# A graph kernel on one core: every second scatter burst as four 128x32 matmuls a step, and half of a table entry made one tile later

## The chip, the cores and the metric

The kernel runs on one core of a Trainium2 chip. The metric is the device time of one launch in microseconds. The granted TensorE clock is read from the profile of the same execution.

## What is computed

The reference propagates node features seven times along the edges of a random graph (10,000 nodes, 160,000 edges, 128 features), then runs a small attention over the eight versions of each node. The change touches the propagation alone:

```python
h = x                                   # (10000, 128)
toks = [x]
for _ in range(7):
    msg = h[src] * deg_inv_sqrt[src, None] * deg_inv_sqrt[dst, None]
    h = segment_sum(msg, dst, 10000)    # sum of the messages by destination node
    toks.append(h)
tok = stack(toks, axis=1)               # (N, 8, D), then attention, residual, readout
```

## The kernel before

The nodes are cut into 79 tiles of 128. A first stage sorts the edges by cells and builds, for each destination tile, a set of 0/1 matrices in fp8 that is kept in DRAM (`GSd`) and loaded into a tile `w`. Each hop is then matrix work. The features of all nodes lie in SBUF as a table `tab` of f16 values; an entry is 256 wide, a high half and a low half, which together hold a 32-bit value closely enough. There are two such tables, one that a hop reads and one that it writes; a copy in DRAM (`tabd`, and `tabh` for the last seven tiles) serves the few edges that are fetched by index.

Hops 2 to 7 run in the second part of `run`. For each destination tile `block` does the following.

- `gather` (nine calls a tile, L608): four 128x32 matrices of `w`, side by side in the four column groups of TensorE, pick up to 32 rows each out of four source tiles into a quarter of a PSUM tile `p`. A call makes two such groups, so a tile has 18 groups, 72 matmuls. The pool of `p` has six buffers. ScalarE (L613) evacuates five of the nine `p` tiles and VectorE (L615) four, into f16 tiles `eb`.
- `begin` opens the accumulator `acc` with the rows that were fetched by index (`fetched`, L568: two full 128x128 matrices).
- `scat` (L583) multiplies the gathered rows by full 128x128 matrices of `w` and adds them up in `acc`, two matmuls for each `eb`.
- `close` adds the two halves of `acc` on VectorE (L599, the tile `s`) and calls `fin`.

The order on TensorE follows from the list `pend`: a scatter is put there when its gather is issued, and when a tile's nine gathers are out, the list is emptied down to two. So TensorE sees bursts: 72 gather matmuls of one tile, then 20 scatter matmuls (two of `begin`, the last four products of the tile before, and the first fourteen of this one), then the gathers of the next tile. The places in a hop's order are numbered n = 0 to 78 (tiles 72 to 78 first, then 0 to 71).

`fin` makes the new table entry of a finished tile in `entries`: ScalarE writes the high half (L644), VectorE the low half (L645), which is the value less the high half, and the maximum of the tile (L646), from which the next hop's scale comes. `rows` (L168, L172) then stores the entry in DRAM from SyncE's queue, and `token_out` has GpSimd scale `s` (L653) and SyncE store it (L655). The matrices of a later tile are loaded from SyncE's queue too (L783). GpSimd issues the fetches by index (L544).

At the start of a hop the scale is worked out in `scale`, with a few small matmuls (L135, L143) between the bursts of n = 0 and n = 1; these two tiles take their second fetched rows late (L597), because those need the whole table of the hop before in DRAM.

Of the kernel before, what the change touches and what calls it, by code (L numbers as in the profile page):

```python
# [13 lines left out]
ALU = mybir.AluOpType  # L14
X = mybir.AxisListType.X
# [4 lines left out]
NT = 79  # L20
NG = 18
NI = 1
# [25 lines left out]
class Hops:  # L48
# [91 lines left out]
    def spread(self, pp, m, out, tag="acc"):  # L140
        nc = self.nc
        pb = pp.tile([128, 512], F32, name="pb", tag=tag)[:, 0:1]
        nc.tensor.matmul(pb, self.ones32, m, start=True, stop=True)  # L143
        nc.vector.tensor_copy(out, pb)
# [401 lines left out]
        return o  # L546

    def block(self, t, w, tab, og, pend, lag, runs, first, evac, fin, lead=False, late=False, mid=None, ahead=None,
              after=None):

        nc, V, A, T, G = self.nc, self.nc.vector, self.nc.scalar, self.nc.tensor, self.nc.gpsimd
        acc = []

        def both(W, rows, start, ones):

            T.matmul(acc[0][:, :128 + ones], W, rows[:, 128:256 + ones], start=start, stop=False, skip_group_check=True)  # L558
            T.matmul(acc[0][:, :128], W, rows[:, :128], start=False, stop=False, skip_group_check=True)  # L559


        def fetched(i, start=False, stop=False):
            W = w[:, (NG + i) * 128:(NG + i + 1) * 128] if i < NI else self.Sov[:, t, :]
            if first:
                both(W, og[i], False, 0)
                T.matmul(acc[0][:, 128:129], W, self.ones16, start=False, stop=stop, skip_group_check=True)  # L566
                return
            T.matmul(acc[0][:, :256], W, og[i], start=start, stop=stop)  # L568

        def begin():  # L570
            acc.append(self.pacc.tile([128, 512], F32, name="acc", tag="acc"))
            for i in range(NI if late else NI + 1):
                fetched(i, start=i == 0)

        def scat(e, jj):
            if not acc:
                acc.append(self.pacc.tile([128, 512], F32, name="acc", tag="acc"))
            for j in range(e.shape[1]):
                J = 2 * jj + j
                if first:  # L580
                    both(w[:, J * 128:(J + 1) * 128], e[:, j], J == 0, 1)
                else:
                    T.matmul(acc[0][:, :256], w[:, J * 128:(J + 1) * 128], e[:, j, :256], start=False, stop=J == NG - 1 and not late)  # L583
                if first and J == 0 and not lead:
                    for i in range(NI):
                        fetched(i)

        def close():
            if first:
                if lead:  # L590
                    for i in range(NI):
                        fetched(i)
                fetched(NI, stop=True)
                fin(t, acc[0][:, :128], acc[0])
                return
            if late:
                T.matmul(acc[0][:, :256], self.Sov[:, t, :], og[NI], start=False, stop=True)  # L597
            s = self.fp.tile([128, 128], F32, name="s")
            V.tensor_reduce(s, acc[0][:, 0:256].rearrange("p (h d) -> p d h", h=2), axis=X, op=ALU.add)  # L599
            fin(t, s, acc[0])  # L600

        def gather(jj):
            n = min(2, NG - 2 * jj)
            p = self.pg.tile([128, 2, 2, 128], F32, name="p")
            for j in range(n):
                for q in range(4):
                    s = 4 * (2 * jj + j) + q
                    T.matmul(p[32 * q:32 * q + 32, j], w[:, NJ * 128 + s * CAP:NJ * 128 + (s + 1) * CAP], tab[:, s, :], start=True, stop=True)  # L608
            e = self.ebuf[self.eb_i % len(self.ebuf)]
            self.eb_i += 1  # L610
            pv = p[:, :n].rearrange("p j h d -> p j (h d)")
            if evac(jj):
                A.activation(e[:, :n, 0:256], pv, AF.Copy, scale=4.0)  # L613
            else:
                V.tensor_tensor(e[:, :n, 0:256], pv, self.four[:, :, None].to_broadcast([128, n, 256]), op=ALU.mult)  # L615
            pend.append(lambda: scat(e[:, :n], jj))

        jj = 0
        for i, n in enumerate(runs):
            for _ in range(n):  # L620
                gather(jj)
                if jj == 0 and not first and not mid:
                    ahead(self.ebuf[(self.eb_i - 1) % len(self.ebuf)][:, 0, 0:1])
                jj += 1
            if mid:
                mid(0)
            if not first:
                begin()
                if mid:
                    ahead()  # L630
            while len(pend) > lag:
                pend.pop(0)()
            if mid:
                mid(1)
            if after:
                after()
            if i == len(runs) - 1:
                pend.append(close)
            yield

    def entries(self, t, s, i):

        c, new = self.c1[i][:, t:t + 1], self.tab[1 - i]
        self.nc.scalar.activation(new[:, t, 0:128], s, AF.Copy, scale=c)  # L644
        self.nc.vector.scalar_tensor_tensor(new[:, t, 128:256], s, c, new[:, t, 0:128], op0=ALU.mult, op1=ALU.subtract)  # L645
        self.nc.vector.tensor_reduce(self.mx[1 - i][:, t:t + 1], new[:, t, 0:128], axis=X, op=ALU.max, apply_absolute_value=True)  # L646

    def token_out(self, k, t, s, ct):
        r = self.fp.tile([128, 128], F32, name="r")
# [7 lines left out]
    def run(self, ctx, att, nhop=K):  # L657
        tc, nc, V, A, T, G = self.tc, self.nc, self.nc.vector, self.nc.scalar, self.nc.tensor, self.nc.gpsimd
        with ExitStack() as c:
# [35 lines left out]
            dsl, W = [[] for _ in quads], [[] for _ in quads]  # L695
# [30 lines left out]
        with ExitStack() as c:  # L726
# [11 lines left out]
            for k in range(2, nhop + 1):  # L738
                i = 1 - k % 2
# [20 lines left out]

                def fin(t, s, acc, k=k, ct=ct, last=last, i=i):
                    if not last:
                        self.entries(t, s, i)
                        self.rows(1 - i, self.tab[1 - i], t, t + 1, nc.sync)
                    self.token_out(k, t, s, ct)


                order = [*range(4 * NG, NT), *range(4 * NG)]
                og = [[None] * (NI + 1) for _ in order]


                def ahead(n, after=None, og=og, order=order, din=din):
                    if n + 2 < NT:
                        for j in range(NI):
                            og[n + 2][j] = self.fetch(order[n + 2], j, din, after=None if j else after)
                    for m in range(0 if n == 0 else n + 2, min(n + 3, NT) if n >= 0 else 0):
                        og[m][NI] = self.fetch(order[m], NI, din, "ogl" if m < 2 else None)
# [3 lines left out]
                for n, t in enumerate(order):  # L781
                    w = self.gsp.tile([128, (NJ + NG) * 128], F8, name="w")
                    nc.sync.dma_start(w, self.GSd[t])  # L783
                    if k == 2 and n == 20:
                        att.constants(c, self.pg.tile([128, 512], F32, name="aw", tag="p"), self.ident)
                    if last and 40 <= n < 40 + 8 * FIRST:
                        att.load((n - 40) // 8, (n % 8,))

                    after = pend.pop() if n == 1 else None
                    for _ in self.block(t, w, tab, og[n], pend, 2, (9,), False, lambda jj: jj in (0, 2, 4, 5, 7), fin, n == 0, n < 2,  # L790
                                        (lambda part, n=n: scale(part, n)) if n < 2 and not last else None,
                                        lambda after=None, n=n: ahead(n, after), after):
                        pass
                while pend:
                    pend.pop(0)()
# [578 lines left out]
```

## Time and profile before

| | us |
|---|---|
| median of 3 runs | 3949.62 (3941.75 to 3951.11) |
| the profiled execution, its own time | 3958.33 |
| its span, first to last instruction | 3956.4 |
| granted TensorE clock, mean | 0.974 |
| hops 2 to 7 within the span | about 1189 to 3304 |

In the profile, PE is TensorE's matmuls and PEld its weight loads, DVE is VectorE, ACT ScalarE, POOL GpSimd, and SPq the queue of SyncE from which DMAs are issued. A line of the timeline has the start, the time from the first start to the last end of a merged run of instructions, the engine, the line of the code, the operation, the names of what is written and read, the shape and the number of instructions; in brackets stands the idle time of the engine before it and what ended it. A shape such as 128*32 128x256 is a matmul of a matrix of 128 rows and 32 columns. Matmuls overlap and their ends are modelled, so a burst's pace is read from starts. A row of the windows has the stretch, its length, the busy time of PE, PEld, DVE, ACT and POOL with the number of instructions, the granted clock, the share of the DMA engines and GB/s.

### The profile page before, as it was taken

Reading aid. Unit: us, or ns where it says so; the run is one execution under the profiler, and the core shown is the slowest. Engines: PE = TensorE matmul, PEld = TensorE weight load, DVE = VectorE, ACT = ScalarE, POOL = GpSimd, SP = SyncE. Lnnn points to the kernel's source line nnn. Section 1 sums busy time; section 2 is a strip of 40 time slices with the busy share of each in tenths; the row PEclk is TensorE's granted clock in tenths of the full one; section 3 lists DMA queues with packets and bytes.
Section 4 is the critical chain, followed back from the end, with each engine's and each line's share of the span. In section 5 each row is a group of like instructions: output and inputs, shape, how many; then the busy total and the mean of one; then the engine's idle time right before and its main releaser. Section 6 shows DMA issues by size and latency. Waiting matters only on the chain.

```text
span 3956.4 us, 174256 instructions
## 1 busy us (share of the span) xinstructions
PE 3707.2 (94%) x74141; PEld 2992.0 (76%) x74141; DVE 3165.6 (80%) x6888; ACT 2812.9 (71%) x6950; POOL 1689.8 (43%) x2221
## 2 busy tenths in 40 slices
PE   6787899999989999999999999999999998999997
PEld 4665677777768888888888788878878886777775
DVE  8998999998867777777777777777776664888888
ACT  6885577777776666766667677666765657888885
POOL 0000234333345665666566566656656662121111
PEclk8998899999999999999999999999999999999998
DMA  3100454545456666666666666666666653222220
GB/s 101 37 2 1 146 160 152 164 148 158 142 160 191 199 202 194 203 200 203 192 198 203 183 205 203 198 191 198 203 191 202 189 183 98 83 76 84 77 83 18
DMA packets 332729, 595.58 MB, mean 151 GB/s; under 512 B 57447, under 2 KB 215493, under 8 KB 326693
## 3 DMA queue, kind: packets, MB, share of 16 engines
q1 hardware_dynamic: 293989, 506.70, 40.6%
q0 software_dynamic: 35392, 72.55, 6.7%
q8 instruction: 580, 9.50, 1.0%
q10 hardware_dynamic: 2560, 5.12, 0.5%
q14 instruction: 208, 1.70, 0.2%
HBM read 455.49 MB, written 128.67 MB: 148 GB/s over the span
## 4 chain that ended last, share of the span: by engine, by line
PE 72%; DVE 16%; DMA 5%; ACT 3%; issue 2%; SPq 1%; another core or an unknown queue 0%; ACTq 0%; DVEq 0%; POOLq 0%
PE p L608 26%; PE acc L583 23%; PE acc L568 4%; PE pv L1018 4%; PE pu L1002 3%; DMA rb<-srow 2%; DVE o L219 2%; DVE w L532 2%; DVE oh L213 2%; DVE ux L226 2%; PE po L1037 2%; PE tb L449 2%; PE pt L992 2%; PE ps L1067 1%; ACT rs L347 1%
## 5 line engine op out<-in xcount | busy, mean ns | idle before, releaser
L613 ACT ACTIVATE eb<-p 128x512 f16<-128x512 f32 x3065 | 1636.7, 604 | 566.2 <-PE p L608 327.9
L615 DVE TENSOR_TENSOR eb<-p,four 128x512 f16<-128x512 f32 x1912 | 1232.0, 686 | 334.8 <-PE acc L583 201.3
L608 PE MATMUL p<-tab,w 128*32 128x256 f16 x39816 | 1296.2, 275 | 42.8 <-issue 15.3
L608 PEld LDWEIGHTS <-w 128*32 128x32 fp8e4 x39816 | 998.9, 96 | 231.6 <-issue 171.4
L583 PE MATMUL acc<-eb,w 128*128 128x256 f16 x8532 | 1013.6, 273 | 0.7 <-issue 0.7
L583 PEld LDWEIGHTS <-w 128*128 128x128 fp8e4 x8532 | 836.7, 98 | 99.9 <-issue 1.3
L544 POOL DMA_INDIRECT og<-tabh,oidx x553 | 626.1, 1132 | 662.3 <-DVE vi L487 388.3
L544 POOL DMA_INDIRECT og<-tabd,oidx x541 | 553.4, 1023 | 752.2 <-PE acc L566 311.8
L653 POOL TENSOR_SCALAR r<-s,ctok 128x128 f32<-128x128 f32 x474 | 294.9, 622 | 48.7 <-DVE s L599 31.1
L644 ACT ACTIVATE tab<-s,c 128x128 f16<-128x128 f32 x395 | 158.5, 401 | 204.0 <-DVE eb L615 167.7
L645 DVE SCALAR_TENSOR_TENSOR tab<-s,c,tab 128x128 f16<-128x128 f32 x395 | 138.9, 352 | 180.6 <-issue 168.8
L1107 POOL TENSOR_TENSOR p<-e,in 128x1024 f32<-128x1024 f32 (+1 forms) x40 | 76.5, 1913 | 447.0 <-DVE e L1106 447.0
L1059 ACT ACTIVATE junk<-tab 128x128 f32<-128x128 f32 x626 | 248.6, 402 | 8.4 <-SPq L1343 6.8
L347 ACT ACTIVATE rs<-iof,rb 128x128 fp8e4<-128x128 f32 x784 | 231.8, 389 | 0.3
L599 DVE TENSOR_REDUCE s<-acc 128x128 f32<-128x256 f32 x474 | 196.8, 415 | 24.8 <-PE acc L597 11.7
L558 PE MATMUL acc<-eb,w 128*128 128x129 f16 x1422 | 214.5, 225 | 1.8 <-ACT eb L613 1.7
L532 DVE TENSOR_TENSOR w<-dsl,iof 128x2432 fp8e4<-128x2432 f16 x79 | 211.9, 2683 | 0.8 <-PE acc L559 0.8
L559 PE MATMUL acc<-eb,w 128*128 128x128 f16 x1422 | 210.7, 222 | 0.0
L558 PEld LDWEIGHTS <-w 128*128 128x128 fp8e4 x1501 | 140.1, 98 | 65.8 <-issue 62.9
L543 POOL COPY og<-eb 128x1 f16<-128x1 f16 x452 | 84.1, 186 | 240.2 <-ACT eb L613 240.1
L1018 PEld LDWEIGHTS pv<-Wv,xT 128*64 128x64 f32 x2504 | 138.9, 137 | 44.7 <-ACT uT L1003 29.1
L1018 PE MATMUL pv<-Wv,xT 128*64 128x131 f32 x2504 | 163.6, 280 | 8.4 <-issue 4.6
(299 smaller groups left out, 5048.7 us busy)
## 6 DMA issues: line engine op xcount, KB each, us to landing
w<-gsd SPq DMA_DIRECT2D x474, 592.0 KB
gsd<-w SPq DMA_DIRECT2D x79, 592.0 KB
tok<-r SPq DMA_DIRECT2D x546, 64.0 KB
tab<-tok SPq DMA_DIRECT2D x273, 128.0 KB
tabd<-tab SPq DMA_DIRECT2D x396, 64.0 KB
ra<-srow SPq DMA_DIRECT2D x79, 320.0 KB
rb<-srow SPq DMA_DIRECT2D x79, 256.0 KB
og<-tabh,oidx POOLq DMA_INDIRECT x553
```

The costliest lines, as they stand in the source:

```text
L347: A.activation(ro[:, j - a, i, :], self.iof, AF.Abs_reciprocal_sqrt, scale=2.0 ** 21, bias=rb[:, j - VP, i:i + 1], saturate=False)
L532: V.tensor_tensor(w[:, :NJ * 128].rearrange("p (j d) -> p j d", d=128), dsl[:, g, :, None].to_broadcast([128, NJ, 128]), self.iof1[:, None ...
L544: self.nc.gpsimd.indirect_dma_start(out=o, out_offset=None, in_=src[0] if i == NI else src[1], in_offset=bass.IndirectOffsetOnAxis(ap=self ...
L558: T.matmul(acc[0][:, :128 + ones], W, rows[:, 128:256 + ones], start=start, stop=False, skip_group_check=True)
L559: T.matmul(acc[0][:, :128], W, rows[:, :128], start=False, stop=False, skip_group_check=True)
L583: T.matmul(acc[0][:, :256], w[:, J * 128:(J + 1) * 128], e[:, j, :256], start=False, stop=J == NG - 1 and not late)
L608: T.matmul(p[32 * q:32 * q + 32, j], w[:, NJ * 128 + s * CAP:NJ * 128 + (s + 1) * CAP], tab[:, s, :], start=True, stop=True)
L613: A.activation(e[:, :n, 0:256], pv, AF.Copy, scale=4.0)
L615: V.tensor_tensor(e[:, :n, 0:256], pv, self.four[:, :, None].to_broadcast([128, n, 256]), op=ALU.mult)
L653: self.nc.gpsimd.tensor_scalar(r, s, ct[:, t:t + 1], None, op0=ALU.mult)
L1018: T.matmul(p[64 * h:64 * h + 64, u - us[0], :], S[i]["xT"][:, h * m + q, 64 * c:64 * c + 64], Wv, start=True, stop=True, tile_position=(0, ...
L1059: A.activation(j, S[i]["x"][:, g, :], AF.Square, bias=S[i]["x"][:, g, 0:1], scale=-1.0, accum_out=R[i % 6][:, 0, g:g + 1])
```

## The change

Two edits. First, `block` gets a flag `narrow`, which is set for every odd place n of a hop. `begin` writes it to the object, so that it holds from the opening of one tile's accumulator to the opening of the next. While it holds, each scatter matmul of a full 128x128 matrix and 256 columns of data is replaced by four with 32 columns of the matrix each, in the four column groups, which write their quarters of the same accumulator. The sum is the same.

Second, `entries` no longer makes the low half and the maximum at once: it returns them, with the row store, as a function that `fin` puts in a list and calls when the next tile is finished (at the hop's last tile all that is left is called).

```diff
+        def spread(W, rows, start, stop):
+
+            if not self.narrow:
+                T.matmul(acc[0][:, :256], W, rows, start=start, stop=stop)
+                return
+            for q in range(4):
+                T.matmul(acc[0][32 * q:32 * q + 32, :256], W[:, 32 * q:32 * q + 32], rows, start=start, stop=stop,
+                         tile_position=(0, 32 * q))
 
         def begin():
+            self.narrow = narrow
...
-            T.matmul(acc[0][:, :256], W, og[i], start=start, stop=stop)
+            spread(W, og[i], start, stop)
...
-                    T.matmul(acc[0][:, :256], w[:, J * 128:(J + 1) * 128], e[:, j, :256], start=False, stop=J == NG - 1 and not late)
+                    spread(w[:, J * 128:(J + 1) * 128], e[:, j, :256], False, J == NG - 1 and not late)
...
-                T.matmul(acc[0][:, :256], self.Sov[:, t, :], og[NI], start=False, stop=True)
+                spread(self.Sov[:, t, :], og[NI], False, True)
...
         self.nc.scalar.activation(new[:, t, 0:128], s, AF.Copy, scale=c)
-        self.nc.vector.scalar_tensor_tensor(new[:, t, 128:256], s, c, new[:, t, 0:128], op0=ALU.mult, op1=ALU.subtract)
-        self.nc.vector.tensor_reduce(self.mx[1 - i][:, t:t + 1], new[:, t, 0:128], axis=X, op=ALU.max, apply_absolute_value=True)
+
+        def rest():
+            self.nc.vector.scalar_tensor_tensor(new[:, t, 128:256], s, c, new[:, t, 0:128], op0=ALU.mult, op1=ALU.subtract)
+            self.nc.vector.tensor_reduce(self.mx[1 - i][:, t:t + 1], new[:, t, 0:128], axis=X, op=ALU.max, apply_absolute_value=True)
+            self.rows(1 - i, new, t, t + 1, self.nc.sync)
+
+        return rest
...
                     if not last:
-                        self.entries(t, s, i)
-                        self.rows(1 - i, self.tab[1 - i], t, t + 1, nc.sync)
+                        rest.append(self.entries(t, s, i))
                     self.token_out(k, t, s, ct)
+                    while len(rest) > (t != order[-1]):
+                        rest.pop(0)()
...
                                         (lambda part, n=n: scale(part, n)) if n < 2 and not last else None,
-                                        lambda after=None, n=n: ahead(n, after), after):
+                                        lambda after=None, n=n: ahead(n, after), after, n % 2 == 1):
```

More of the change, by code (lines that the diff above doesn't have):

```diff
@@ L548, in block @@
     def block(self, t, w, tab, og, pend, lag, runs, first, evac, fin, lead=False, late=False, mid=None, ahead=None,
-              after=None):
+              after=None, narrow=False):
         nc, V, A, T, G = self.nc, self.nc.vector, self.nc.scalar, self.nc.tensor, self.nc.gpsimd
@@ L762, in fin @@
                     if not last:
-                        self.entries(t, s, i)
-                        self.rows(1 - i, self.tab[1 - i], t, t + 1, nc.sync)
+                        rest.append(self.entries(t, s, i))
                     self.token_out(k, t, s, ct)
-                order = [*range(4 * NG, NT), *range(4 * NG)]
+                    while len(rest) > (t != order[-1]):
+                        rest.pop(0)()
+                order, rest = [*range(4 * NG, NT), *range(4 * NG)], []
                 og = [[None] * (NI + 1) for _ in order]
```

## The prediction

> **What bounds the kernel now.** I read the page first, then the windows of 100 us, then the timeline of a few tiles of one hop, then the list of waits and the timeline around the end of a hop.
>
> ```profile
> span 3956.4 us, 174256 instructions
> PE 3707.2 (94%) x74141; PEld 2992.0 (76%) x74141; DVE 3165.6 (80%) x6888; ACT 2812.9 (71%) x6950; POOL 1689.8 (43%) x2221
> L608 PE MATMUL p<-tab,w 128*32 128x256 f16 x39816 | 1296.2, 275 | 42.8 <-issue 15.3
> L583 PE MATMUL acc<-eb,w 128*128 128x256 f16 x8532 | 1013.6, 273 | 0.7 <-issue 0.7
> ...
> 1400.00:1500.00 100.00, 100.00 (x2100) 84.67 (x2096) 78.04 (x161) 70.01 (x139) 63.92 (x92) 1.00 0.64 202
> ...
> 1890.00:2243.00 353.00, 349.70 (x7275) 294.37 (x7273) 272.22 (x566) 240.86 (x474) 218.74 (x313) 1.00 0.64 198
> ```
>
> Each of the six hops 2 to 7 lasts about 353 us, and inside one TensorE counts as busy all the time (100.00 of 100 us, granted clock 1.00) while VectorE has 78, ScalarE 70, GpSimd 64 and the DMA share is 0.64. So TensorE sets the pace, and the question is whether all of its 100 us is work. The timeline of one tile answers it:
>
> ```profile
> 1402.63 0.41 DVE L599 TENSOR_REDUCE s<-acc 128x128 f32<-128x256 f32 x1
> 1403.08 0.40 ACT L644 ACTIVATE tab<-s,c 128x128 f16<-128x128 f32 x1 [1.02 <-DVE eb L615]
> 1403.26 1.87 PEld L608 LDWEIGHTS <-w 128*32 128x32 fp8e4 x72 [0.21 <-issue]
> 1403.26 2.15 PE L608 MATMUL p<-tab,w 128*32 128x256 f16 x72
> 1403.52 0.35 DVE L645 SCALAR_TENSOR_TENSOR tab<-s,c,tab 128x128 f16<-128x128 f32 x1 [0.47 <-issue]
> 1403.78 2.07 ACT L613 ACTIVATE eb<-p 128x512 f16<-128x512 f32 x4 [0.29 <-PE p L608]
> 1403.79 0.28 DVE L646 TENSOR_REDUCE mx<-tab 128x1 f32<-128x128 f16 x1
> 1404.01 1.89 DVE L615 TENSOR_TENSOR eb<-p,four 128x512 f16<-128x512 f32 x3
> 1405.34 0.28 PE L568 MATMUL acc<-og,w 128*128 128x256 f16 x1
> 1405.46 0.27 PE L568 MATMUL acc<-og,Sov 128*128 128x256 f16 x1
> 1405.57 2.13 PE L583 MATMUL acc<-eb,w 128*128 128x256 f16 x18
> 1407.63 2.15 PE L608 MATMUL p<-tab,w 128*32 128x256 f16 x72
> ```
>
> A tile is a gather burst (L608: 18 groups of four 128x32 matrices) and a scatter burst (L568 and L583: 20 full 128x128 matrices), together 1407.63 - 1403.26 = 4.37 us. Steps inside a burst: L583's 18 take 2.13 us, so (2.13 - 0.273) / 17 = 0.109 us each; L608's 18 groups take (2.15 - 0.275) / 17 = 0.110 us each. So four narrow matmuls side by side cost what one full matmul costs, and 38 steps make 38 x 0.109 = 4.15 us. The missing 0.22 us a tile sit at the two changes of width: 1405.34 - 1403.26 = 2.08 us against 18 x 0.109 = 1.96 (0.12 lost going to wide), and 1407.63 - 1405.34 = 2.29 against 20 x 0.109 = 2.18 (0.11 lost going to narrow). TensorE's busy column hides them, because the modelled tail of a matmul (273 ns) covers the gap.
>
> Is it the change of width, and not the change of operands, of accumulator or of line? The attention stage has both cases:
>
> ```profile
> 3504.76 0.40 PE L1073 MATMUL sm<-lb,same 128*32 128x128 f32 x8
> 3504.98 1.06 PE L1226 MATMUL pf<-tab,Ab 128*32 128x128 f32 x32
> 3505.97 1.10 PE L1037 MATMUL po<-v,t 64*64 64x128 f32 x32
> ...
> 3514.94 1.44 PE L1067 MATMUL ps<-xT,uT 128*32 128x32 f32 x128
> ...
> L1067 PE MATMUL ps<-xT,uT 128*32 128x32 f32 x5008 | 56.2, 199 | 1.8 <-issue 1.6 <-ACT uT L1003 0.2
> L1226 PE MATMUL pf<-tab,Ab 128*32 128x128 f32 x1252 | 45.5, 288 | 0.9 <-ACT ry L1160 0.9
> ```
>
> L1073's two groups of four begin 3504.98 - 3504.76 = 0.22 us ahead of L1226: 0.11 a group, so narrow to narrow, with other operands and another target, loses nothing. L1226 to L1037 (32 columns to 64x64) takes 3505.97 - 3504.98 = 0.99 us for 8 groups: 0.99 - 8 x 0.109 = 0.12 lost. The loss goes with the width.
>
> **The change, part by part.** (1) In the odd places of a hop's order (n = 1, 3 ... 77: 39 of 79, six hops, 234 bursts) the scatter becomes narrow. The switch is set where the burst opens, so the leftovers of the tile before (its last four products) turn narrow too and the whole burst of 20 has one width. Gather, scatter, gather are then one run: both changes of width around it go, 468 in all. In hops 2 to 6 a small full-height matmul still stands between the second gather and its scatter:
>
> ```profile
> 1541.23 0.35 PE L143 MATMUL pb<-r,ones 1*128 1x1 f32 x2 [0.19 <-DVE r L156]
> ```
>
> That gives 5 changes back: 463 x 0.11 = 51 us gained.
>
> (2) What a narrow scatter costs: 20 x 4 matmuls and 20 x 4 weight loads for 20 and 20. Time by L608's step: 0.110 against 0.109, so 20 x 0.001 = 0.02 us a burst, 5 us in all if that last digit is real. L608 writes fresh, though, and the scatter accumulates. The row that accumulates in narrow groups is L1226 (its two halves r = 0, 1 add into one place): (1.06 - 0.29) / 7 = 0.110 a group. So accumulating costs no more; I take 0 and keep 0 to 5 us. The weight loads (0.097 each in the row x72, side by side for four column groups) hide behind the matmuls as they do in the gather. The Trainium skill (TensorEngine Tiling (Array Packing), Restrictions) says that column tiling switches off the fast weight load, which speaks against this part. By that rule the loads of a group could outlast its matmuls; the gather's 0.110 with the same loads shows that they don't, and the sum by the rule stays the same.
>
> (3) More instructions: 234 x 20 x 3 = 14,040 matmuls and as many weight loads, 28,080. Rows for their supply:
>
> ```profile
> q8 instruction: 580, 9.50, 1.0%
> ...
> 2496.84 1.37 PE L608 MATMUL p<-tab,w 128*32 128x256 f16 x41
> 2498.44 0.64 PE L608 MATMUL p<-tab,w 128*32 128x256 f16 x15 [0.22 <-issue]
> 2499.32 0.62 PE L608 MATMUL p<-tab,w 128*32 128x256 f16 x16 [0.25 <-issue]
> 2499.88 0.28 PE L568 MATMUL acc<-og,w 128*128 128x256 f16 x1
> ...
> 2739.12 0.53 PE L608 MATMUL p<-tab,w 128*32 128x256 f16 x10 [0.37 <-issue]
> ```
>
> 580 packets for 2 x 74,141 instructions are 256 instructions a packet; 28,080 more are 110 packets, 1.8 MB, nothing for the DMA. But some gathers halt with nothing to wait for: this one takes 2499.88 - 2496.84 = 3.04 us instead of 2.08. The next such pair begins 2739.12 - 2498.44 = 241 us later; at 256 instructions a packet and 42 instructions a us (2100 + 2096 in the 100 us quoted first) that is near 40 packets. If they go by packets, 110 more bring 3 more, 3 x 0.96 = 3 us (bounds 0 and 10).
>
> (4) The low half of a table entry (L645), its maximum (L646) and its row store move one tile later. Now VectorE stands 0.47 us in front of L645 for ScalarE's L644; queued behind it are L646 and the evacuation L615. Then the half in hand is a tile old and waits for nothing: L645 starts at 1403.04 instead of 1403.52. This matters because of (1): with the gap gone the gather starts 0.11 earlier, so its second group wants L615 at about 1403.90, while today's order frees VectorE at 1403.79 + 0.28 = 1404.07. In the new order it is free at about 1403.67. That cover gone, the gain would shrink as in the first rival. On SyncE the row store now stands behind the token store L655 (which waits for GpSimd's scaling L653), ahead of the next load of matrices L783:
>
> ```profile
> 1404.31 0.38 SPq L655 DMA_DIRECT2D tok<-r  x1
> 1406.49 0.32 SPq L783 DMA_DIRECT2D w<-gsd  x1
> ```
>
> The queue is free for 1406.49 - 1404.69 = 1.8 us there, and the store needs 0.32. `s` is kept one tile longer, with four buffers.
>
> (5) The end of a hop pays: the last two entries are finished together, just when the next hop's first gather needs the last table tiles.
>
> ```profile
> 1534.73 2.34 PE L608 MATMUL p<-tab,w 128*32 128x256 f16 x72
> 1534.91 0.42 DVE L599 TENSOR_REDUCE s<-acc 128x128 f32<-128x256 f32 x1 [0.41 <-PE acc L583]
> 1536.16 0.35 DVE L645 SCALAR_TENSOR_TENSOR tab<-s,c,tab 128x128 f16<-128x128 f32 x1
> 1536.43 0.28 DVE L646 TENSOR_REDUCE mx<-tab 128x1 f32<-128x128 f16 x1
> 1536.96 0.38 SPq L655 DMA_DIRECT2D tok<-r  x1
> 1541.59 0.95 POOL L544 DMA_INDIRECT ogl<-tabd,oidx  x1 [3.02 <-DMA tok<-r]
> 1545.73 0.27 PE L597 MATMUL acc<-ogl,Sov 128*128 128x256 f16 x1 [1.97 <-DMA ogl<-tabd,oidx]
> ```
>
> One more L645 and L646 (0.35 + 0.28 = 0.63 us) and one more row store (0.32 us in the same queue) come ahead of the last store, for which the late fetch and then L597 wait. Bounds 0 and 0.95 us, five times; part of it fits into the wait for L644, so I take 0.4 x 5 = 2 us.
>
> Sum: -51 + 0 + 3 + 2 = -46 us. The profiled execution (3958.3 us, span 3956.4) would become 3912; it lies 8.7 us above the median of the runs shown, 3949.6, and from that I predict 3904. VectorE stays off the bound: 78% of 4.37 is 3.4 us of work in a tile of 4.15.
>
> **Rivals.** *Evacuation takes the gap's place.* There are six p tiles for nine products, so the eighth waits until the second is evacuated: L615 ends it at 1404.01 + 0.69 = 1404.70, and the eighth starts at 1403.26 + 7 x 0.22 = 1404.80. The margin is 0.1 us. If VectorE comes late by as much as is won at the change back to gathering, 234 x 0.11 = 26 us of the 51 return: about 3930. For it: the small margin; against it: part (4), and ScalarE's free time before L613 (0.29). Chance 0.11.
>
> *The change does not do what it says: a narrow accumulating scatter is slower per step.* At 0.120 instead of 0.109 us, 20 x 0.011 x 234 = 51 us eat the whole gain: 3950, no change. L1226 (0.110) speaks against it, though it is f32 with 128 columns a pass. Chance 0.05.
>
> *Slower: TensorE runs short of instructions.* The place is the run of 18 + 20 + 18 groups, 8 instructions each 0.109 us, 6.1 us long instead of 2.08. If each such run met one halt like that at 2498 (0.96 us), 234 x 0.96 = 225 us come on top: 3904 + 225 = 4129. It decides from one halt in five runs on (46 / 0.96 = 48 halts). Against it: L1067 issues 128 narrow pairs in 1.44 us, (1.44 - 0.20) / 256 = 4.8 ns an instruction, so 8 take 39 ns; a packet of 256 lasts 3.5 us at the narrow pace, and in the 100 us window quoted first the gathers do not slow towards their end. For it: the halts exist, and their cause isn't shown. Chance 0.08. The Trainium skill (Runtime: NRT & Kernel Launch, Instruction fetch mechanics) gives an issue floor of about 20 cycles an instruction; at the 1.2 GHz that its page TensorE: Matmul & The Clock Gate (Part 1) gives for the sequencer, an estimate from both, eight would take 0.133 us, the 56 groups of a run 56 x 0.024 = 1.3 us more, and the kernel about 4210. L1067's 4.8 ns and the gather's own 0.110 disagree; of the 0.08 it has 0.01.
>
> **How the numbers follow.** The forecast has 0.76. A measurement of this kernel tells about 0.3%, 12 us, from no change. Forecast and first rival are faster by more: 0.87; the second is no change: 0.05; the third slower: 0.08. The range: below, 51 us and 2 more for the last digit of the gap with none of the costs, and the runs' own spread of some 4 us, 3893; above, the first rival, 3932.
>
> **What would show it.** Two tiles in a row take 8.52 us instead of 8.73: around an odd scatter the bursts start 1.97 us (gather to scatter) and 2.18 us (scatter to gather) apart, around an even one 2.08 and 2.29 as now. Matmuls 74,141 become about 88,200, q8 packets about 690. The idle 0.47 before L645 is gone. Wrong would be: narrow scatter steps above 0.115 us; `PE p` waiting for `DVE eb`; new "issue" gaps in the odd bursts; a hop that ends more than 1 us later than now.

## The result: 4144 us, slower than the kernel before

| | before | changed |
|---|---|---|
| median, us | 3949.39 (3941.75 to 3951.11, 4 runs) | 4144.24 (4137.15 to 4147.92, 4 runs) |
| span of the profiled execution, us | 3956.4 | 4142.7 |
| granted TensorE clock, mean | 0.974 | 0.972 |

The ratio is 1.0499 (95% interval 1.0486 to 1.0511): 195 us slower, where 46 us faster was forecast. The page of the changed kernel, its span, the engines, the costliest lines of TensorE and the instruction queue:

```profile
span 4142.7 us, 202335 instructions
PE 3779.6 (91%) x88181; PEld 3099.8 (75%) x88181; DVE 3177.0 (77%) x6888; ACT 2812.8 (68%) x6950; POOL 1690.1 (41%) x2221
...
q8 instruction: 690, 11.30, 1.1%
...
L618 PE MATMUL p<-tab,w 128*32 128x256 f16 x39816 | 1309.2, 275 | 36.5 <-ACT eb L623 13.5
...
L576 PE MATMUL acc<-eb,w 128*32 128x256 f16 x16848 | 622.7, 273 | 133.5 <-issue 120.1
L576 PEld LDWEIGHTS <-w 128*32 128x32 fp8e4 x17784 | 488.1, 96 | 252.7 <-issue 246.7
L573 PE MATMUL acc<-eb,w 128*128 128x256 f16 x4320 | 512.4, 273 | 1.8 <-issue 1.8
```

The counts are the forecast ones (88,181 matmuls, 690 packets). New is idle time of TensorE ahead of the narrow scatter L576, put down to "issue": it waited for nothing that the profile shows. The same two windows as before:

```profile
1400.00:1500.00 100.00, 94.16 (x2570) 81.77 (x2561) 71.89 (x147) 63.62 (x126) 57.81 (x84) 1.00 0.58 186
1890.00:2243.00 353.00, 329.48 (x8776) 284.41 (x8769) 249.85 (x517) 219.29 (x433) 198.66 (x285) 0.99 0.58 182
```

TensorE is busy for 94 of 100 us instead of 100, and every other engine and the transfers are slower in proportion, so it is TensorE that loses the time. One pair of tiles in the timeline (lines in between left out):

```profile
1406.33 2.15 PE L618 MATMUL p<-tab,w 128*32 128x256 f16 x72
...
1407.96 1.02 POOL L544 DMA_INDIRECT og<-tabh,oidx  x1 [0.27 <-POOL og L543]
...
1408.30 0.28 PE L576 MATMUL acc<-og,w 128*32 128x256 f16 x4
...
1409.24 1.18 PEld L576 LDWEIGHTS <-w 128*32 128x32 fp8e4 x43 [0.40 <-issue]
1409.35 0.60 ACT L623 ACTIVATE eb<-p 128x512 f16<-128x512 f32 x1 [0.45 <-PE acc L576]
1409.71 0.96 POOL L544 DMA_INDIRECT og<-tabd,oidx  x1 [0.73 <-PE acc L576]
...
1411.06 0.63 PE L576 MATMUL acc<-eb,w 128*32 128x256 f16 x16 [0.39 <-issue]
...
1411.49 2.33 PE L618 MATMUL p<-tab,w 128*32 128x256 f16 x72
...
1413.75 0.28 PE L573 MATMUL acc<-og,w 128*128 128x256 f16 x1
...
1416.04 1.17 PE L618 MATMUL p<-tab,w 128*32 128x256 f16 x36
```

Gather to odd scatter takes 1408.30 - 1406.33 = 1.97 us, as forecast: the change of width costs nothing any more. Odd scatter to gather takes 1411.49 - 1408.30 = 3.19 us where 2.18 was forecast: two halts, about 0.4 and 0.6 us. Each ends 1.3 us after the start of one of GpSimd's two indirect fetches (1407.96 + 1.3 = 1409.26; 1409.71 + 1.3 = 1411.01). The evacuation L623 at 1409.35 tells the same: the gather that it reads had ended by 1408.5 (1406.33 + 2.15), and the word of it came 0.9 us later. Neither halt waits for evacuated rows: the first is over before this evacuation begins, and the second begins at about 1410.4, after it has ended (1409.35 + 0.60). The pair takes 1416.04 - 1406.33 = 9.71 us instead of 8.73.

### The profile page after: what moved, and what is told of

It is laid out like the page before. It is cut to its first block, busy times and chain, and to the rows that moved or that the text cites. A ratio compares the mean times of both kernels' runs of the same rounds, so it can differ in the third digit from the quotient of the medians.

```text
span 4142.7 us, 202335 instructions
## 1 busy us (share of the span) xinstructions
PE 3779.6 (91%) x88181; PEld 3099.8 (75%) x88181; DVE 3177.0 (77%) x6888; ACT 2812.8 (68%) x6950; POOL 1690.1 (41%) x2221
## 4 chain that ended last, share of the span: by engine, by line
PE 72%; DVE 15%; issue 5%; DMA 4%; ACT 4%; SPq 0%; ACTq 0%; DVEq 0%
PE p L618 25%; PE acc L576 15%; PE acc L573 13%; PE pv L1034 3%; PE pu L1018 3%; DVE w L532 2%; DMA rb<-srow 2%; ACT rs L347 2%; PE po L1053 2%; DVE oh L213 2%; PE pt L1008 2%; DVE ux L226 2%; PE tb L449 2%; DVE o L219 2%; DVE R L219 1%
## 5 line engine op out<-in xcount | busy, mean ns | idle before, releaser
L623 ACT ACTIVATE eb<-p 128x512 f16<-128x512 f32 x3065 | 1637.5, 604 | 754.3 <-PE p L618 548.2
L618 PEld LDWEIGHTS <-w 128*32 128x32 fp8e4 x39816 | 1044.9, 97 | 158.8 <-issue 103.2
L544 POOL DMA_INDIRECT og<-tabh,oidx x553 | 627.3, 1134 | 662.1 <-DVE vi L487 389.0
L544 POOL DMA_INDIRECT og<-tabd,oidx x541 | 552.8, 1022 | 734.6 <-PE acc L566 301.3
L576 PE MATMUL acc<-eb,w 128*32 128x256 f16 x16848 | 622.7, 273 | 133.5 <-issue 120.1
L576 PEld LDWEIGHTS <-w 128*32 128x32 fp8e4 x17784 | 488.1, 96 | 252.7 <-issue 246.7
L573 PEld LDWEIGHTS <-w 128*128 128x128 fp8e4 x4560 | 445.3, 98 | 103.8 <-issue 54.5
L573 PE MATMUL acc<-eb,w 128*128 128x256 f16 x4320 | 512.4, 273 | 1.8 <-issue 1.8
L654 ACT ACTIVATE tab<-s,c 128x128 f16<-128x128 f32 x395 | 158.4, 401 | 206.2 <-DVE eb L625 165.9
L657 DVE SCALAR_TENSOR_TENSOR tab<-s,c,tab 128x128 f16<-128x128 f32 x395 | 139.5, 353 | 180.5 <-issue 170.7
L558 PEld LDWEIGHTS <-w 128*128 128x128 fp8e4 x1501 | 139.9, 98 | 65.7 <-issue 62.8
```

Source lines behind the costliest of these rows:

```text
L544: self.nc.gpsimd.indirect_dma_start(out=o, out_offset=None, in_=src[0] if i == NI else src[1], in_offset=bass.IndirectOffsetOnAxis(ap=self ...
L573: T.matmul(acc[0][:, :256], W, rows, start=start, stop=stop)
L576: T.matmul(acc[0][32 * q:32 * q + 32, :256], W[:, 32 * q:32 * q + 32], rows, start=start, stop=stop, tile_position=(0, 32 * q))
```

## The experiments

Two theories. The **rate theory** is the forecast's third rival: eight instructions every 0.109 us are more than TensorE can be supplied with, so narrow bursts halt by themselves. The **fetch theory**: for about 1.2 us after GpSimd starts an indirect fetch (L544), TensorE receives no new instructions and its semaphore updates do not come out; what it has in hand outlasts that in a wide burst, not in a narrow one. In the expectations on chip 6 the fetch theory is called theory one or blocked supply, and the rate theory is theory two. On chips 8 and 4 it is the other way round: theory one is the rate theory and theory two the fetch theory.

Twelve runs, some of them of the same kernel, were made in three groups, each group on one chip at one time, with the kernel before beside it. All ratios are to that kernel before. Chips 6 and 4 behave alike; chip 8 repeats the result above.

| kernel | chip | median, us | before there, us | ratio, 95% interval |
|---|---|---|---|---|
| second edit alone, wide | 6 | 3916.13 | 3916.34 | 0.9994 (0.9983 to 1.0006) |
| narrow every fourth | 6 | 3904.38 | 3916.34 | 0.9966 (0.9954 to 0.9978) |
| narrow, plain fetches | 6 | 3895.72 | 3916.34 | 0.993 (0.9906 to 0.9955) |
| wide, plain fetches | 6 | 3904.1 | 3916.34 | 0.9961 (0.9947 to 0.9975) |
| changed, unaltered | 8 | 4142.51 | 3949.32 | 1.0486 (1.0462 to 1.0511) |
| narrow alone | 8 | 4144.49 | 3949.32 | 1.0486 (1.0462 to 1.051) |
| narrow, one indirect fetch | 8 | 3986.66 | 3949.32 | 1.0091 (1.0067 to 1.0115) |
| narrow, plain fetches | 8 | 3913.0 | 3949.32 | 0.9897 (0.9868 to 0.9927) |
| wide, plain fetches | 4 | 3911.8 | 3919.64 | 0.9975 (0.9965 to 0.9986) |
| narrow, plain fetches, no loads | 4 | 3863.09 | 3919.64 | 0.9853 (0.9835 to 0.9871) |
| narrow every fourth | 4 | 3907.59 | 3919.64 | 0.9974 (0.9959 to 0.9989) |
| changed, unaltered | 4 | 3901.16 | 3919.64 | 0.9949 (0.9929 to 0.9969) |

**First group, chip 6.** *The second edit alone*, all bursts wide:

```diff
-                                        lambda after=None, n=n: ahead(n, after), after, n % 2 == 1):
+                                        lambda after=None, n=n: ahead(n, after), after, False):
```

> The second edit alone: every scatter burst is wide as before, the low half, maximum and row store are made one tile later. Theory one (blocked supply): for about 1.2 us from the start of each of GpSimd's indirect fetches TensorE gets no new instructions; a wide burst lives on what is queued, a narrow one runs dry. No narrow scatter here, so no loss: 3950 us, at most 5 more for the hop ends. Theory two (rate): TensorE's instruction supply sustains only some 50 a us on average, whatever GpSimd does: 3950 too. Theory three (narrow step): a narrow accumulating scatter itself halts: 3950 too. If the late half is the cause of the loss, which no theory says, it is near 4144.

It measured 0.9994: the edit brings nothing and costs nothing. But the low half isn't late in what ran. VectorE's order in this trace is that of the kernel before but for one swap at the first tile of each of hops 2 to 6, an evacuation ahead of the maximum; on SyncE alone the row store now stands behind the token store. The changed kernel has the same order. At the end of a hop, where two low halves should stand together, and at the start of the next, where the first tile should have none, its timeline shows one each:

```profile
1559.69 0.42 DVE L609 TENSOR_REDUCE s<-acc 128x128 f32<-128x256 f32 x1 [0.42 <-PE acc L573]
...
1560.95 0.35 DVE L657 SCALAR_TENSOR_TENSOR tab<-s,c,tab 128x128 f16<-128x128 f32 x1
1561.21 0.28 DVE L658 TENSOR_REDUCE mx<-tab 128x1 f32<-128x128 f16 x1
...
1574.24 0.42 DVE L609 TENSOR_REDUCE s<-acc 128x128 f32<-128x256 f32 x1 [6.32 <-PE acc L576]
...
1575.74 0.34 DVE L657 SCALAR_TENSOR_TENSOR tab<-s,c,tab 128x128 f16<-128x128 f32 x1
```

Why the program came out in this order is not shown. So this run measures the order of the stores, and no run has a low half made a tile later.

*Narrow at every fourth tile:* `n % 4 == 1` in place of `n % 2 == 1`, and the flag `skip_group_check=True` on the scatter matmuls.

> Narrow scatter in every fourth place (n = 1, 5 ... 77: 20 a hop, 120 in all) instead of every second. Blocked supply and narrow step: each narrow burst costs what it cost with 234 of them, 195 / 234 = 0.83 us net, so 120 x 0.83 = 100 us: about 4050. Rate: four tiles then need 4 x 144 + 3 x 40 + 160 = 856 instructions in 17.2 us, 49.8 a us, where the changed kernel's pairs sustained 488 in 9.7 us, 50.3: nothing runs dry, and 120 bursts win their 0.22 us: about 3925.

0.9966: faster, where the fetch theory wanted some 100 us more than the kernel before. A miss; the rate theory's 25 us less came nearer, with 12 measured. The narrow bursts of this trace ran without the two halts although the fetches went on as before. The kernel before, too, was 33 us faster on this chip than where the result was taken, so the question became what was different here.

*Plain fetches:* SyncE copies fixed rows instead of the rows that the index names, in hops 2 to 7; first with narrow odd bursts, then with all bursts wide.

```diff
+        if hasattr(self, "c1"):
+            a = (4 * NG - 1) * 128 if i == NI else (NT - 4 * NG - 1) * 128
+            self.nc.sync.dma_start(o, src[0 if i == NI else 1][a:a + 128, :])
+            return o
         self.nc.gpsimd.indirect_dma_start(out=o, out_offset=None, in_=src[0] if i == NI else src[1],
```

> The changed kernel; in hops 2 to 7 the two fetches by index of a tile are replaced by plain DMAs of the same size (128 fixed rows of 512 bytes, so the fetched rows are not the right ones) from SyncE's queue, same tiles, same gate and same waits. Blocked supply: the halts in the narrow bursts (0.41 and 0.66 us, 234 of each, some 245 us) go, and those at the hop starts too: 3870 to 3900. Rate: 4144 as before. Traffic (instruction packets that stand behind the loads of matrices and fetched rows): the same bytes move, 4144. Narrow step: 4144.

> As the run with plain fetches, but every scatter wide (fixed rows are fetched, not those by index). It is the base for that run: blocked supply says that the halts at the hop starts and the pairs every 240 us go, 3910 to 3945, and that the run with narrow scatters and plain fetches is 45 to 55 us below it (463 changes of width of 0.11 us less small costs). Rate and narrow step: the narrow one is about 195 us above it.

0.993 and 0.9961. Narrow bursts brought 8 us over wide ones, not the 45 to 55 that were expected, even without any indirect fetch; that is taken up in the third group. What differs from the first two traces shows in a count over 1200 to 3200 us of each trace: how many of TensorE's instructions that update a semaphore ended 0.2 to 1.2 us after an indirect fetch had started, how many updates appeared in that time, and how often TensorE halted for over 0.25 us beyond a step's 0.109.

```
                            ends  updates   halts, us in all
before (first trace)        1744       55     45    29.7
changed (first trace)       1369       32    432   201.0
second edit alone, chip 6   1773     1383     11    14.4
every fourth, chip 6        1801     1411     21    17.0
changed, chip 8             1373       34    431   200.7
changed, chip 4             1794     1284     48    36.4
```

In the two first traces the updates all but stop (32 for 1369) while a fetch is made; on chip 6 they go on (1411 for 1801). I call this the stop. In the changed kernel's first trace the middle half of the halts begin 0.66 to 0.89 us after a fetch's start and end 1.29 to 1.32 us after it. Instruction packets show no such fixed distance: in the middle half one had landed 1.3 to 4.8 us before a halt's end. The stop is in the trace of before as well, where it costs little.

**Second group, chip 8.** *The changed kernel unaltered, and the first edit alone* (`self.entries(t, s, i)()`: the low half at once).

> The changed kernel, unaltered, timed once more beside the kernel before. Theory one (the odd bursts are short of instructions whatever else goes on, 1.07 us of halts a pair) gives the ratio 1.05 again, 234 x 1.07 us of halts less the width changes saved. Theory two (the halts come from the 1.2 us after the start of each indirect fetch, in which TensorE's semaphore updates stopped in the two first traces and did not in the trace with every fourth burst narrow) makes the time depend on whether that stop shows: where it shows, 1.05 and two halts in each narrow burst; where TensorE's updates go on beside the fetches, no halts and 463 x 0.11 us less than before, less what the plain-fetch kernel lost elsewhere: a ratio of 0.985 to 0.995.

> The narrow odd bursts alone: a table entry's low half is made at once, as before the change. Both theories give the time of the changed kernel within 0.3%, 1.05 of the kernel before where narrow bursts halt and 0.985 to 0.995 where they don't, since the late low half alone measured 0.9994. If the late low half had been what made room for the narrow bursts, or what stopped them, this one stands apart from the changed kernel by over 0.5%.

Both 1.0486, and the stop is there (34 updates for 1373 ends). TensorE's instructions are the same in both, and the loss is the narrow bursts' alone.

*One of the two indirect fetches plain* (the copy above, only for `i == NI`).

> The changed kernel with one of a tile's two indirect fetches of hops 2 to 7, the one from the table of late rows, replaced by a plain transfer of fixed rows, so those rows are the wrong ones. Theory two: where the stop shows, one of the two halts is left in each narrow burst and the ratio falls from 1.05 to about half way, 1.00 to 1.03 (4144 less 234 x 0.41 to 0.66 us); where it doesn't show, 0.985 to 0.995. Theory one: both halts stay, 1.05.

3986.66 us, where 4144 - 234 x 0.66 = 3990 was the lower price. Its timeline has the one halt that belongs to the fetch which is left, and not the other:

```profile
1400.83 1.02 POOL L548 DMA_INDIRECT og<-tabh,oidx  x1 [0.27 <-POOL og L543]
...
1401.17 0.28 PE L580 MATMUL acc<-og,w 128*32 128x256 f16 x4
...
1402.13 1.57 PEld L580 LDWEIGHTS <-w 128*32 128x32 fp8e4 x58 [0.41 <-issue]
1402.15 1.83 PE L580 MATMUL acc<-eb,w 128*32 128x256 f16 x58
...
1403.72 2.22 PE L622 MATMUL p<-tab,w 128*32 128x256 f16 x72
```

From 1401.17 to 1403.72 are 2.55 us: 2.18 and one halt. The halt ends at 1402.13, 1.30 after the fetch's start, and the last 58 matmuls run through.

*Both plain, beside the others.*

> Both indirect fetches of hops 2 to 7 replaced by plain transfers of fixed rows (the rows are the wrong ones), timed beside the unaltered changed kernel. Theory two: no halts at all, 0.985 to 0.995 of the kernel before, whether or not the others halt. Theory one: the halts stay, 1.05.

3913.0 us, 0.9897. On one chip, then, the instructions of TensorE being the same, two indirect fetches a tile give 4142.5, one 3986.7, none 3913.0. The rate theory is out as the cause of the slowdown; the fetches are the cause where the stop shows. The plain copies take away GpSimd's work for a fetch (1.02 us) and its transfer together, so which of the two holds TensorE up is not shown.

**Third group, chip 4.** *Wide with plain fetches, again:*

> All bursts wide, both indirect fetches of hops 2 to 7 replaced by plain transfers of fixed rows (the wrong ones), timed beside the changed kernel. Theory two: where TensorE's updates stop after each indirect fetch, taking the fetches away also frees the wide kernel, and it comes to the time that it has where nothing stops, about 3904 us, a ratio near 0.9885; where nothing stops, 0.996 as before. If the fetches cost a wide kernel nothing, 0.996 on either. Beside it the narrow plain-fetch kernel's 0.9897 shows what narrow bursts alone bring: 463 width changes would be 51 us under this one.

There is no stop in this group (1284 updates for 1794 ends in the changed kernel), and it measured 0.9975, near the 0.996 of the other chip without it. What it would be on a chip with the stop was not run. *Narrow, plain fetches, and no matrix loads after the first five tiles:*

```diff
-                    w = self.gsp.tile([128, (NJ + NG) * 128], F8, name="w")
-                    nc.sync.dma_start(w, self.GSd[t])
+                    if k == 2 and n < 5:
+                        wkeep.append(self.gsp.tile([128, (NJ + NG) * 128], F8, name="w"))
+                        nc.sync.dma_start(wkeep[n], self.GSd[t])
+                    w = wkeep[n % 5]
```

> The changed kernel with plain fetches of fixed rows, and with the 592 KB matrix loads of hops 2 to 7 left out after the first five tiles of hop 2 (five tiles' matrices are used in turn), so the rows and the matrices are the wrong ones. In the plain-fetch kernel some 60 halts of 0.35 us and more were left in hops 2 to 7, 43 us in all, each ending about 1.4 us after a 16 KB instruction packet had landed. If those packets come late because they share the transfer engines with the matrix loads, the halts go here, and the whole 51 us of the width changes show: about 3904 - 51 = 3853 us, a ratio of 0.975 to 0.985. If the supply of instructions is late by itself, whatever else is transferred, they stay and the time is that of the plain-fetch kernel, 0.989 to 0.994.

3863.09 us, 48.7 under the wide kernel with plain fetches on the same chip: this is the 51 us of the width changes, nearly whole (the ratio is 0.0003 past the expected end). A wide kernel without loads was not run, but the wide one with loads has only 1.4 us of halts to lose. The windows of 400 us, first the narrow plain-fetch kernel of chip 6, then this one (the first row of each, and the sums):

```profile
1200.00:1600.00 400.00, 392.92 (x11065) 354.34 (x11057) 309.21 (x655) 269.25 (x546) 70.80 (x178) 1.00 0.70 203
...
sum 2000.00, PE 1968.82 PEld 1775.63 DVE 1510.85 ACT 1325.90 POOL 356.59; mean PE 393.76 PEld 355.13 DVE 302.17 ACT 265.18 POOL 71.32
```

```profile
1200.00:1600.00 400.00, 399.79 (x11333) 363.31 (x11331) 316.67 (x671) 274.95 (x559) 72.92 (x182) 1.00 0.24 67
...
sum 2000.00, PE 1997.02 PEld 1817.08 DVE 1538.43 ACT 1348.68 POOL 366.55; mean PE 399.40 PEld 363.42 DVE 307.69 ACT 269.74 POOL 73.31
```

With the loads (DMA share 0.70) TensorE misses 6 us in 400, without them (0.24) under one. The wide kernel with loads misses hardly any: 4 halts and 1.4 us in these 2000 us, against 56 and 39.4 for the narrow one (57 and 37.2 on chip 8), and 9 and 4.3 for the narrow one without loads. The halts of the narrow one end in the median 1.44 us after an instruction packet of queue q8 had landed (the middle half 1.35 to 1.50; a random moment 1.1 to 3.5). The halts of the unaltered changed kernel on chip 4 do so too, in the median after 1.42 us. So they are taken to be late instructions: at the narrow pace a packet is used up every 3.5 us, and beside the matrix loads some come too late. The Trainium skill (Runtime: NRT & Kernel Launch, Instruction fetch mechanics) says that a 16 KiB block is fetched while the one before is executed, and that this is mostly hidden; here it is hidden for the wide kernel, and for the narrow one but for those 39 us.

*Every fourth, and the changed kernel once more:*

> Every fourth burst narrow, indirect fetches as before. Theory two: where TensorE's updates stop after each fetch, half of the changed kernel's cost or a little more: about 117 x 1.07 us of halts less 230 x 0.11 us of width changes, 100 us over the kernel before, a ratio of 1.025; where they don't stop, 0.9966 as measured earlier. A theory in which what decided was how often bursts are narrow, and not the stop, gives 0.9966 on either.

> The changed kernel, unaltered, beside the kernel before and the others of this call. Theory two: 1.049 where the stop shows in its trace; where it doesn't, as every fourth burst narrow measured 0.9966 there and the narrow plain-fetch kernel 0.993, a ratio of 0.985 to 0.997. Theory one: 1.049 on either.

0.9974 and 0.9949. The unaltered changed kernel, 5% slower on chip 8, is 18.5 us faster than the kernel before on chip 4, and of the kernels that do the whole computation it is the fastest there. Its timeline has the same fetches, at the same places:

```profile
1600.65 2.15 PE L618 MATMUL p<-tab,w 128*32 128x256 f16 x72
1602.28 1.02 POOL L544 DMA_INDIRECT og<-tabh,oidx  x1 [0.27 <-POOL og L543]
...
1602.62 0.28 PE L576 MATMUL acc<-og,w 128*32 128x256 f16 x4
...
1602.73 1.96 PEld L576 LDWEIGHTS <-w 128*32 128x32 fp8e4 x72
1602.84 2.14 PE L576 MATMUL acc<-eb,w 128*32 128x256 f16 x72
1603.60 0.94 POOL L544 DMA_INDIRECT og<-tabd,oidx  x1 [0.30 <-PE acc L576]
1604.67 0.43 DVE L657 SCALAR_TENSOR_TENSOR tab<-s,c,tab 128x128 f16<-128x128 f32 x1 [0.47 <-ACT tab L654]
...
1604.80 2.14 PE L618 MATMUL p<-tab,w 128*32 128x256 f16 x72
...
1606.88 0.28 PE L573 MATMUL acc<-og,w 128*128 128x256 f16 x1
...
1609.16 2.15 PE L618 MATMUL p<-tab,w 128*32 128x256 f16 x72
```

The 72 narrow matmuls run through beside two fetches: 1604.80 - 1602.62 = 2.18 us, and the pair 1609.16 - 1600.65 = 8.51. The same distances as medians over all tiles of hops 2 to 7, from the starts in each trace, in us:

| | gather to odd scatter | odd scatter to gather | pair |
|---|---|---|---|
| before, first trace | 2.08 | 2.29 | 8.74 |
| changed, first trace | 1.97 | 3.19 | 9.59 |
| one indirect fetch, chip 8 | 1.97 | 2.55 | 8.97 |
| plain fetches, chip 8 | 1.97 | 2.18 | 8.52 |
| changed, chip 4 | 1.97 | 2.18 | 8.52 |
| plain, no loads, chip 4 | 1.97 | 2.18 | 8.52 |

What stays open is what sets the stop. Chip 8 and the first traces have it, 6 and 4 have not; each group ran on one chip at one time, so whether it belongs to the chip or to a setting of it at that time can't be told. That TensorE's queue empties is read from "issue" and from the place of the halts; the queue itself is not in a trace.

## Why the prediction was wrong, point by point

- **Step 1, the width changes (-51 us): right.** 1.97 and 2.18 us around an odd scatter, and on chip 4 2.07 and 2.29 around an even one, are what was said, and 234 pairs x (8.74 - 8.52) = 51 us. The kernel with nothing in its way shows 48.7 of them.
- **Step 2, the narrow step's cost (0): right.** 20 steps in 2.18 us are 0.109 each. The Trainium skill (TensorEngine Tiling (Array Packing), Restrictions) says that column tiling switches off the fast weight load; that has no cost here. The Trainium skill (Runtime: NRT & Kernel Launch, Instruction fetch mechanics) has an issue floor, 0.133 us for eight instructions as the prediction estimated it; these 0.109 disagree.
- **Step 3, more instructions (+3 us, bounds 0 to 10): this is the step that failed, twice.** Where the result was taken, its halts are 234 x (9.59 - 8.52) = 250 us, and 250 - 51 = 199 is the loss (195 measured). Their cause was none that the step weighed: not packets but GpSimd's fetches. The halt from which it took its price seems to belong with these as well (below the list). The second failure is of size: late packets cost not 3 us but 39 in the narrow plain-fetch kernel, and on chip 4 the changed kernel's halts of 36.4 us (14.4 with all bursts wide on chip 6) leave some 29 of the 51 us; 18.5 were measured. Most of the 10 between lie in delays too short for this count: by the mean distance of a pair, which has them all, it is 234 x (8.83 with all bursts wide on chip 6 - 8.74 on chip 4) = 21 us.
- **Step 4, the late low half: wrong in what it does; what it is worth was not measured.** The half in hand was to be a tile old; in what ran, L657 still follows the same tile's L654, with 0.47 us of idle VectorE ahead of it: 180.5 us in all, as before (180.6). So the cover that the step counted on never came. Nothing needed it either: with plain fetches and no loads the pair is at 8.52, so the evacuation does not take the gap's place (**first rival**: no). The second rival's 0.120 us a step: no.
- **Step 5, the hop's end (+2 us):** the second edit alone measured 0.9994, but the two last entries were not finished together in it, so the cost that the step named was not put to the test.
- **Third rival (0.08): the right engine, the right symptom and nearly the right time (4129 against 4144), the last by luck.** It reckoned with one halt of 0.96 us in each run and left its cause open; nearly every odd burst met two, of about 0.4 and 0.6 us (3.19 - 2.18 = 1.01), which happen to add up to nearly the same, and a stop that it had not thought of made them. The evidence set against it, L1067's 4.8 ns and the gather's steady pace, was blind to this: a gather is over or nearly over when a fetch begins (on chip 4 at 1602.28 and 1603.60, about a scatter that opens at 1602.62), and the attention stage of L1067 makes none.

The trace of before had two signs. The first is in the halt that step 3 priced, the one that ends at 2498.44. A gather's fetch mostly starts when the gather is nearly over; here one starts at its beginning:

```profile
2496.94 0.96 POOL L544 DMA_INDIRECT og<-tabd,oidx  x1 [0.30 <-issue]
```

The trace has six such pairs of halts, at multiples of about 240 us. Their first halts begin 0.86 to 1.02 us after a fetch's start and end 1.49 to 1.55 us after it; the last packet had landed 1.8 to 6.6 us before, at no fixed distance. With all bursts wide on chip 6 there is no such pair. So they too seem to come with the stop, and they do not go by packets; the second halt of each pair, which ends 0.3 to 0.4 us after the next fetch's start, is not explained.

The second sign is a wait. On the page VectorE's evacuation stands idle 201.3 us for a scatter, not for the gather whose tile it reads; below it the same line with the second edit alone on chip 6:

```profile
L615 DVE TENSOR_TENSOR eb<-p,four 128x512 f16<-128x512 f32 x1912 | 1232.0, 686 | 334.8 <-PE acc L583 201.3
```

```profile
L625 DVE TENSOR_TENSOR eb<-p,four 128x512 f16<-128x512 f32 x1912 | 1190.4, 682 | 304.1 <-PE p L618 300.9
```

The scatter put down as the releaser isn't what the evacuation reads, and the scatter that last read its `eb` buffer lies well back (14 buffers, nine products a tile). So the wait meant that TensorE's word came late, by 0.48 us in the mean (201.3 us, 421 times). With the changed kernel's trace it gives a price: its halts begin 0.66 to 0.89 us after a fetch's start, so with the updates gone from about 0.15 us on TensorE lives for 0.5 to 0.75 us on what it holds, an estimate of 37 to 55 instructions at eight per 0.109 us. In wide bursts as many last 2.0 to 3.0 us, longer than the stop; in narrow ones not.

## What to carry to other kernels

When an edit multiplies an engine's instructions, ask not only whether the mean rate can be supplied but how long the engine can run on what it holds, and what interrupts the supply: here another engine's indirect fetches on chip 8, and late instruction packets beside the matrix loads on all three chips. A wait that the profile puts down to work that the waiting instruction does not read is a finding; follow it before pricing anything beside it. And time a change on more than one chip before it is called slower or faster: this one measured 1.0486 on one and 0.9949 on another. Look in the trace, too, whether an edit has changed the order that an engine runs: the second edit here had not changed VectorE's as meant.

## What the runs showed of the hardware

- In some traces, those of chip 8 and the first two, TensorE gives out hardly any semaphore update 0.2 to 1.2 us after GpSimd starts an indirect fetch (32 of 1369 due in the first trace of the changed kernel; on chip 4 1284 of 1794), at the same granted clock (0.975 on chip 8, 0.974 on chip 4). The kernel before takes 3949 us with this and 3916 to 3920 without.
- A change of matmul width between 32 and 128 columns costs TensorE 0.11 us each way (2.08 against 1.97 us, 2.29 against 2.18), and four 32-column matmuls side by side follow one another at 0.109 us when their instructions are there.
- Instruction packets (16 KB, 256 instructions) come late at the narrow pace while matrix loads keep the transfer engines at 0.70: 56 halts and 39.4 us in 2000 us on chip 6, 9 and 4.3 with the loads left out on chip 4.
